# Interleaving the attention of one batch with the feed-forward chunks of the batch before it, and making the v transposes one chunk ahead

## The chip, the cores and the metric

One core of a Trainium2 chip runs the whole program. The metric is the device time in microseconds (us) of one execution, as the median of several. All the executions compared here of one kernel lie within about 0.3% of each other, so differences of a microsecond or two mean something. The profile is one further look at an execution, taken by the hardware profiler; its span (954.9 us for the kernel before) is about 1.5 us shorter than the device time, because it runs from the first to the last instruction.

The engines are PE (matmul), DVE (vector), ACT (scalar, activation functions), POOL (nearly unused here: a broadcast for each batch) and SP, which issues the loads and stores. PSUM is the memory that PE's matmuls write into; copying a result out of it is called evacuation. A *border* is the stretch in which PE finishes one batch's feed-forward and starts the next one's.

## The reference

Cross-covariance attention over channels, then a SwiGLU feed-forward block:

```python
# q, k, v: (4, 6016, 256) float32; tau = 1
qn = q / (norm(q, axis=1) + 1e-6)
kn = k / (norm(k, axis=1) + 1e-6)
s  = kn.transpose(0, 2, 1) @ qn / tau          # 256 x 256 for each of 4 batches
a  = softmax(s, axis=-1)
x  = (v @ a).reshape(24064, 256)
g  = x @ w_gate                                # 256 -> 1536
out = (silu(g) * (x @ w_val)) @ w_out          # 1536 -> 256
```

Two stages follow from it for each batch. *Attention* reads all of q and k (12.3 MB a batch) to form a 256 x 256 matrix of sums (the prediction calls them Gram sums); it moves many bytes and needs few matmuls. *Feed-forward* needs only v, the weights and that matrix; it has many matmuls and moves few bytes. The kernel never forms `v @ a`: it multiplies the softmax into the gate and value weights once per batch ("folding": `awg`, `awv`), so that feed-forward multiplies v by the folded weights.

## The kernel before

Attention for all four batches comes first, in a scope of its own; feed-forward for all four follows. The parts that matter:

```python
# --- stage 1: attention, all batches (weights loaded first, cast to bf16 on DVE) ---
nc.sync.dma_start(wg_f, ...); nc.sync.dma_start(wv_f, ...); nc.sync.dma_start(wo_f, ...)
for b in range(B):
    ktq_ps = attn_psum.tile([P, CB, C], FP32, tag="ktq")      # 2 KB per partition
    diag_ps = attn_psum.tile([P, 4, P], FP32, tag="diag")     # 2 KB per partition
    for ch in range(12):                                       # 512 rows of q and k
        # load qf, kf; cast qt on ACT (L102) and kt on DVE (L103)
        for t in range(nb):                                    # 128 rows: six matmuls
            # 2 x ktq += kt^T qt (256 columns), 4 x diag += qt^T qt, kt^T kt (128 columns)
            ...
    # the chain: diagonal -> sqrt -> 1/norm -> scale -> max -> exp -> softmax a_sb -> transpose aT
    ...
    for (w_sb, aw) in ((wg_sb, awg_all[b]), (wv_sb, awv_all[b])):    # folding
        for ib in range(CB):
            for fo in range(0, F, 512):
                # 2 matmuls of 512 columns into aw_ps, then:
                nc.scalar.copy(aw[:, ib, fo:fo + 512], aw_ps)

# --- stage 2: feed-forward, all batches, chunks of 512 rows ---
def do_chunk(b, n0, nn):
    # load vf, cast vb on ACT
    # 8 transposes of vb into vT_ps (L46), copied to vT by DVE (L213)
    for fb in range(12):
        # 2 matmuls g_ps (L220), 2 matmuls va_ps (L225), 512 columns each
        nc.scalar.activation(sg[:, :nn], g_ps[:, :nn], AF.Silu)
        nc.vector.tensor_mul(hT[:, fb, :nn], sg[:, :nn], va_ps[:, :nn])
    # 48 matmuls o_ps (L240), 256 columns each, copied by ACT, stored
```

The code carries no order between engines: a scheduler in the language orders each engine's instructions, and the engines then run their own lists in order and wait for each other by semaphores.

Of the kernel before, what the change touches and what calls it, by code (L numbers as in the profile page):

```python
# [9 lines left out]
FP32 = mybir.dt.float32  # L10
# [7 lines left out]
def kernel(  # L18
# [19 lines left out]
    QKCH = 512  # L38
    n_full = N // CHUNK
    rem = N - n_full * CHUNK  # L40
# [8 lines left out]
    const = ctx.enter_context(tc.tile_pool(name="const", bufs=1))  # L49
    ident = const.tile([P, P], BF16)  # L50
# [4 lines left out]
    wo_sb = const.tile([P, FB, D], BF16)  # L55

    aw_pool = ctx.enter_context(tc.tile_pool(name="aw", bufs=1))
# [5 lines left out]
    with tc.tile_pool(name="stg", bufs=1) as stg, \  # L63
         tc.tile_pool(name="qkf", bufs=4) as qkf_pool, \
         tc.tile_pool(name="qkb", bufs=4) as qkb_pool, \
         tc.tile_pool(name="attn_psum", bufs=1, space=bass.MemoryType.PSUM) as attn_psum, \
         tc.tile_pool(name="attn_ps2", bufs=2, space=bass.MemoryType.PSUM) as attn_ps2, \
         tc.tile_pool(name="attn_sb", bufs=2) as attn_sb:

        wg_f = stg.tile([P, CB, F], FP32)  # L70
        wv_f = stg.tile([P, CB, F], FP32)
        wo_f = stg.tile([P, FB, D], FP32)
        nc.sync.dma_start(wg_f, moe_w_gate.rearrange("(cb p) f -> p cb f", p=P))
        nc.sync.dma_start(wv_f, moe_w_val.rearrange("(cb p) f -> p cb f", p=P))
        nc.sync.dma_start(wo_f, moe_w_out.rearrange("(fb p) d -> p fb d", p=P))
        nc.vector.tensor_copy(wg_sb, wg_f)
        nc.vector.tensor_copy(wv_sb, wv_f)
        nc.vector.tensor_copy(wo_sb, wo_f)

        nqk = N // QKCH  # L80
        qk_rem = N - nqk * QKCH

        for b in range(B):
            ktq_ps = attn_psum.tile([P, CB, C], FP32, tag="ktq")
            diag_ps = attn_psum.tile([P, 4, P], FP32, tag="diag")

            ti = 0
            for ch in range(nqk + (1 if qk_rem else 0)):
                n0 = ch * QKCH
                nn = min(QKCH, N - n0)  # L90
                nb = nn // P
                qf = qkf_pool.tile([P, 4, C], FP32, tag="qf")
                kf = qkf_pool.tile([P, 4, C], FP32, tag="kf")
                nc.sync.dma_start(  # L94
                    qf[:, :nb, :],
                    q[b, n0:n0 + nn, :].rearrange("(t p) c -> p t c", p=P))
                nc.sync.dma_start(  # L97
                    kf[:, :nb, :],
                    k[b, n0:n0 + nn, :].rearrange("(t p) c -> p t c", p=P))
                qt = qkb_pool.tile([P, 4, C], BF16, tag="qt")  # L100
                kt = qkb_pool.tile([P, 4, C], BF16, tag="kt")
                nc.scalar.copy(qt[:, :nb, :], qf[:, :nb, :])  # L102
                nc.vector.tensor_copy(kt[:, :nb, :], kf[:, :nb, :])  # L103
                for t in range(nb):
                    st = (ti == 0)
                    sp = (ti == N // P - 1)
                    for ci in range(CB):
                        nc.tensor.matmul(  # L108
                            ktq_ps[:, ci, :],
                            kt[:, t, ci * P:(ci + 1) * P], qt[:, t, :],  # L110
                            start=st, stop=sp, skip_group_check=True)
                    for ci in range(CB):
                        nc.tensor.matmul(  # L113
                            diag_ps[:, ci, :],
                            qt[:, t, ci * P:(ci + 1) * P],
                            qt[:, t, ci * P:(ci + 1) * P],
                            start=st, stop=sp, skip_group_check=True)
                    for ci in range(CB):
                        nc.tensor.matmul(  # L119
                            diag_ps[:, 2 + ci, :],  # L120
                            kt[:, t, ci * P:(ci + 1) * P],
                            kt[:, t, ci * P:(ci + 1) * P],
                            start=st, stop=sp, skip_group_check=True)
                    ti += 1

            diag_vals = attn_sb.tile([P, 4], FP32, tag="diagv")
            scratch = attn_sb.tile([P, P], FP32, tag="scratch")
            for s in range(4):
                nc.vector.tensor_tensor_reduce(  # L129
                    out=scratch, in0=diag_ps[:, s, :], in1=ident,  # L130
                    scale=1.0, scalar=0.0, op0=ALU.mult, op1=ALU.add,
                    accum_out=diag_vals[:, s:s + 1])
            normv = attn_sb.tile([P, 4], FP32, tag="normv")
            nc.scalar.activation(normv, diag_vals, AF.Sqrt)
            rnorm = attn_sb.tile([P, 4], FP32, tag="rnorm")
            nc.vector.reciprocal(rnorm, normv)
            rnorm_b = attn_sb.tile([P, 4], BF16, tag="rnorm_b")
            nc.vector.tensor_copy(rnorm_b, rnorm)

            qn_ps = attn_ps2.tile([P, 1024], BF16, tag="attn_post")  # L140
            for ci in range(CB):
                transpose(qn_ps[0:1, ci * P:(ci + 1) * P],
                          rnorm_b[:, ci:ci + 1], ident)
            qn_row = attn_sb.tile([1, C], FP32, tag="qn_row")
            nc.scalar.activation(qn_row, qn_ps[0:1, :C], AF.Copy,
                                 bias=0.0, scale=inv_tau)
            qn_bc = attn_sb.tile([P, C], FP32, tag="qn_bc")
            nc.gpsimd.partition_broadcast(qn_bc, qn_row)  # L148

            a_sb = attn_sb.tile([P, CB, C], BF16, tag="a_sb")  # L150
            for ci in range(CB):
                srow = attn_sb.tile([P, C], FP32, tag="srow")
                nc.scalar.activation(srow, ktq_ps[:, ci, :], AF.Copy,  # L153
                                     bias=0.0, scale=rnorm[:, 2 + ci:3 + ci])
                nc.vector.tensor_mul(srow, srow, qn_bc)
                nsmax = attn_sb.tile([P, 1], FP32, tag="nsmax")
                nc.vector.reduce_max(nsmax, srow, axis=AX.X, negate=True)
                ssum = attn_sb.tile([P, 1], FP32, tag="ssum")
                esr = attn_sb.tile([P, C], FP32, tag="esr")
                nc.scalar.activation(esr, srow, AF.Exp, bias=nsmax,  # L160
                                     accum_out=ssum)
                rsum = attn_sb.tile([P, 1], FP32, tag="rsum")
                nc.vector.reciprocal(rsum, ssum)
                nc.vector.tensor_scalar(a_sb[:, ci, :], esr, rsum,
                                        None, op0=ALU.mult)

            aT_sb = attn_sb.tile([P, CB, C], BF16, tag="aT_sb")
            for cj in range(CB):
                aT_ps = attn_ps2.tile([P, 1024], BF16, tag="attn_post")
                for ci in range(CB):  # L170
                    transpose(aT_ps[:, ci * P:(ci + 1) * P],
                              a_sb[:, ci, cj * P:(cj + 1) * P], ident)
                nc.scalar.copy(aT_sb[:, cj, :], aT_ps[:, :C])

            for (w_sb, aw) in ((wg_sb, awg_all[b]), (wv_sb, awv_all[b])):
                for ib in range(CB):
                    for fo in range(0, F, 512):
                        aw_ps = attn_ps2.tile([P, 512], FP32, tag="attn_post")
                        for jb in range(CB):
                            nc.tensor.matmul(  # L180
                                aw_ps,
                                aT_sb[:, jb, ib * P:(ib + 1) * P],
                                w_sb[:, jb, fo:fo + 512],
                                start=(jb == 0), stop=(jb == CB - 1))
                        nc.scalar.copy(aw[:, ib, fo:fo + 512], aw_ps)  # L185

    with tc.tile_pool(name="v_pool", bufs=3) as v_pool, \
         tc.tile_pool(name="vb_pool", bufs=3) as vb_pool, \
         tc.tile_pool(name="vt_pool", bufs=2) as vt_pool, \
         tc.tile_pool(name="h_pool", bufs=2) as h_pool, \  # L190
# [6 lines left out]
        def do_chunk(b, n0, nn):  # L197
# [11 lines left out]
            for cb in range(CB):  # L209
                for t in range(nb):  # L210
                    transpose(vT_ps[:, cb, t * P:(t + 1) * P],
                              vb[:, t, cb * P:(cb + 1) * P], ident)
# [78 lines left out]
```

## Time and profile before

| | kernel before |
|---|---|
| device time, median | 956.4 us (13 runs, 955.88 to 956.76) |
| span of the profile | 954.9 us |
| first feed-forward matmul | 181.3 us |
| busy: PE, ACT, DVE | 93%, 55%, 49% |
| DMA, 22 to 165 us | full, 349 GB/s to 54 us, then 340 |
| DMA, from 181 us | 58 GB/s |

How to read it: a busy share over the whole span hides that two stages with different limits follow each other. The prediction below shows the slices and windows from which this is read; columns of a window row are its start and end, its length, then for each engine busy time and (x) number of instructions, the granted PE clock, the DMA share and GB/s.

### The profile page before, as it was taken

What the parts mean: (1) busy time and instruction counts of PE and PEld (TensorE: products, weight loads), DVE (VectorE), ACT (ScalarE), POOL (GpSimd) and SP (SyncE); (2) the same over time, 40 slices, a digit from 0 to 9 for tenths busy, and PEclk for the clock granted to TensorE, in tenths of its full rate; (3) what the DMA queues carried; (4) which work ended last, traced back from release to release, by engine and by line L of the source; (5) the groups of instructions that cost most, each with busy time, mean ns of one, the idle gap of its engine ahead of it and who ended that gap; (6) DMA issues with size and microseconds to landing.
All of it is one profiled execution on the core that took longest, in us unless ns stands there. A gap on an engine that the chain in (4) does not pass through costs nothing.

```text
span 954.9 us, 15732 instructions
## 1 busy us (share of the span) xinstructions
PE 886.3 (93%) x6133; PEld 561.1 (59%) x6184; DVE 471.3 (49%) x747; ACT 529.9 (55%) x866; POOL 4.7 (0%) x10
## 2 busy tenths in 40 slices
PE   1777986899999999999999999999999999999998
PEld 1556755465656566656565566556565656565655
DVE  2233232346454555455555645554646454646463
ACT  1375775845564656465555555555556555655454
POOL 0000000000000000000000000000000000000000
PEclk9999998899999999999999999999999999999999
DMA  9999999401220222021202220211122202210011
GB/s 330 349 349 349 347 347 303 117 23 45 62 89 23 89 67 84 23 89 61 85 28 89 67 83 23 90 61 59 52 83 72 76 31 89 62 43 25 23 45 39
DMA packets 101498, 104.30 MB, mean 109 GB/s; under 512 B 3120, under 2 KB 100912, under 8 KB 101424
## 3 DMA queue, kind: packets, MB, share of 16 engines
q1 hardware_dynamic: 101424, 103.30, 34.0%
q8 instruction: 48, 0.79, 0.3%
q14 instruction: 26, 0.21, 0.1%
HBM read 78.64 MB, written 24.64 MB: 108 GB/s over the span
## 4 chain that ended last, share of the span: by engine, by line
PE 79%; issue 12%; DMA 4%; DVE 2%; SPq 2%; ACT 2%; POOL 0%; POOLq 0%; ACTq 0%; DVEq 0%
PE va_ps L225 26%; PE o_ps L240 26%; PE g_ps L220 25%; DMA qf<-in_q_dram 3%; DVE vT L213 2%; SPq L94 1%; PE vT_ps L46 1%; DMA kf<-in_k_dram 1%; SPq L97 0%; ACT vb L205 0%; ACT awg L185 0%; ACT qt L102 0%; ACT awv L185 0%; POOL qn_bc L148 0%; PE aw_ps L180 0%
## 5 line engine op out<-in xcount | busy, mean ns | idle before, releaser
L231 DVE TENSOR_TENSOR hT<-sg,va_ps 128x512 bf16<-128x512 bf16 (+1 forms) x576 | 387.6, 677 | 258.2 <-ACT sg L230 246.9
L230 ACT ACTIVATE sg<-g_ps 128x512 bf16<-128x512 f32 (+1 forms) x576 | 336.8, 589 | 131.4 <-PE g_ps L220 129.4
L225 PE MATMUL va_ps<-vT,awv 128*128 128x512 bf16 (+1 forms) x1152 | 337.4, 374 | 2.4
L220 PE MATMUL g_ps<-vT,awg 128*128 128x512 bf16 (+1 forms) x1108 | 329.2, 374 | 9.3 <-DVE vT L213 7.9
L240 PE MATMUL o_ps<-wo_sb,hT 128*128 128x256 bf16 x2256 | 254.4, 273 | 0.0
L240 PEld LDWEIGHTS <-hT 128*128 128x128 bf16 x2256 | 219.2, 98 | 37.2 <-DVE hT L231 0.5
L225 PEld LDWEIGHTS <-awv 128*128 128x128 bf16 x1152 | 112.5, 98 | 133.6 <-issue 4.3
L220 PEld LDWEIGHTS <-awg 128*128 128x128 bf16 x1152 | 110.7, 98 | 135.7 <-DVE vT L213 11.7
L246 ACT COPY o_sb<-o_ps 128x512 f32<-128x512 f32 x96 | 55.4, 577 | 210.6 <-PE o_ps L240 210.6
L108 PE MATMUL ktq_ps<-qt,kt 128*128 128x256 bf16 x376 | 74.5, 288 | 37.5 <-DVE kt L103 35.8
L102 ACT CAST qt<-qf 128x1024 bf16<-128x1024 f32 (+1 forms) x48 | 49.3, 1028 | 68.3 <-DMA qf<-in_q_dram 68.1
L213 DVE COPY vT<-vT_ps 128x1024 bf16<-128x1024 bf16 (+1 forms) x48 | 30.6, 675 | 102.2 <-PE vT_ps L46 102.2
L103 DVE CAST kt<-kf 128x1024 bf16<-128x1024 f32 (+1 forms) x48 | 33.1, 690 | 88.5 <-DMA kf<-in_k_dram 79.3
L113 PE MATMUL diag_ps<-qt 128*128 128x128 bf16 x376 | 52.6, 226 | 5.6 <-DVE diag_vals L129 4.3
L108 PEld LDWEIGHTS <-kt 128*128 128x128 bf16 x376 | 30.7, 102 | 43.8 <-DVE kt L103 39.3
L119 PE MATMUL diag_ps<-kt 128*128 128x128 bf16 x376 | 54.2, 226 | 1.1 <-DVE kt L103 1.0
L205 ACT CAST vb<-vf 128x1024 bf16<-128x1024 f32 (+1 forms) x48 | 47.4, 1030 | 2.2 <-DMA vf<-in_v_dram 2.0
L113 PEld LDWEIGHTS <-qt 128*128 128x128 bf16 x376 | 35.6, 101 | 14.1 <-ACT qt L102 5.4
L119 PEld LDWEIGHTS <-kt 128*128 128x128 bf16 x376 | 31.8, 102 | 4.6 <-DVE kt L103 1.5
L46 PE MATMUL vT_ps<-ident,vb 128*128 128x128 bf16 x376 | 26.7, 226 | 1.3 <-ACT srow L153 1.2
L46 PEld LDWEIGHTS <-vb 128*128 128x128 bf16 x376 | 24.4, 101 | 2.4 <-issue 1.7
L180 PEld LDWEIGHTS <-aT_sb 128*128 128x128 bf16 x96 | 9.0, 97 | 12.6 <-issue 6.3
(36 smaller groups left out, 110.8 us busy)
## 6 DMA issues: line engine op xcount, KB each, us to landing
qf<-in_q_dram SPq DMA_DIRECT2D x44, 512.0 KB, 8.8
kf<-in_k_dram SPq DMA_DIRECT2D x44, 512.0 KB, 8.8
vf<-in_v_dram SPq DMA_DIRECT2D x44, 512.0 KB, 4.8
out_dram<-o_sb SPq DMA_DIRECT2D x44, 512.0 KB, 3.0
wg_f<-in_moe_w_gate_dram SPq DMA_DIRECT2D x1, 1536.0 KB, 6.9
wv_f<-in_moe_w_val_dram SPq DMA_DIRECT2D x1, 1536.0 KB, 10.7
wo_f<-in_moe_w_out_dram SPq DMA_DIRECT2D x1, 1536.0 KB, 14.7
qf<-in_q_dram SPq DMA_DIRECT2D x4, 384.0 KB, 8.6
```

What stands on the lines that cost most here:

```text
L46: nc.tensor.matmul(out_ap, in_ap, ident_ap, is_transpose=True, start=True, stop=True, skip_group_check=True)
L102: nc.scalar.copy(qt[:, :nb, :], qf[:, :nb, :])
L108: nc.tensor.matmul(ktq_ps[:, ci, :], kt[:, t, ci * P:(ci + 1) * P], qt[:, t, :], start=st, stop=sp, skip_group_check=True)
L113: nc.tensor.matmul(diag_ps[:, ci, :], qt[:, t, ci * P:(ci + 1) * P], qt[:, t, ci * P:(ci + 1) * P], start=st, stop=sp, skip_group_check=True)
L119: nc.tensor.matmul(diag_ps[:, 2 + ci, :], kt[:, t, ci * P:(ci + 1) * P], kt[:, t, ci * P:(ci + 1) * P], start=st, stop=sp, skip_group_chec ...
L213: nc.vector.tensor_copy(vT[:, :, :nn], vT_ps[:, :, :nn])
L220: nc.tensor.matmul(g_ps[:, :nn], awg[:, cb, fb * P:(fb + 1) * P], vT[:, cb, :nn], start=(cb == 0), stop=(cb == CB - 1))
L225: nc.tensor.matmul(va_ps[:, :nn], awv[:, cb, fb * P:(fb + 1) * P], vT[:, cb, :nn], start=(cb == 0), stop=(cb == CB - 1))
L230: nc.scalar.activation(sg[:, :nn], g_ps[:, :nn], AF.Silu)
L231: nc.vector.tensor_mul(hT[:, fb, :nn], sg[:, :nn], va_ps[:, :nn])
L240: nc.tensor.matmul(o_ps[:, t - t0, :], hT[:, fb, t * P:(t + 1) * P], wo_sb[:, fb, :], start=(fb == 0), stop=(fb == FB - 1), skip_group_che ...
L246: nc.scalar.copy(o_sb[:, t0:t1, :], o_ps[:, :t1 - t0, :])
```

## The change

Its intent is to let PE do feed-forward of batch b while the q and k of batch b+1 are loaded, and to take the copy of the transposed v out of PE's path. Its core, cut:

```diff
-        for b in range(B):                      # all of attention first
-            ...                                  # loads, sums, chain, folding
-        for b in range(B):                      # then all of feed-forward
-            for ci in range(n_full):
-                do_chunk(b, ci * CHUNK, CHUNK)
+    for (dst, src, shp) in ((wg_sb, ...), (wv_sb, ...)):   # gate and value weights first
+        ...
+    alloc_attn_state(0)
+    for ch in range(n_ch):
+        attn_qk_chunk(0, ch)
+    ...                                          # output weights loaded here
+    attn_post(0)                                 # chain and folding
+    for b in range(B):
+        nb = b + 1
+        for ch in range(n_ch):
+            mid = nb == B - 1 and ch == n_ch - 2
+            if nb < B - 1:
+                attn_qk_chunk(nb, ch)
+                if ch == n_ch - 1:
+                    attn_post(nb)
+            elif nb == B - 1:                    # last attention: a little faster, so that
+                ...                              # its chain falls before the last chunk
+            ffn_chunk(b, ch, last_qk if mid else None)
```

```diff
 def ffn_chunk(b, ch, between=None):
     ...                                          # 48 gate and value matmuls
+    nxt = (b, ch + 1) if ch + 1 < n_ch else (b + 1, 0)
+    if nxt[0] < B:
+        ffn_vt(*nxt)                             # load, cast, transpose v of the next chunk
+    if between:
+        between()
     ...                                          # 48 output matmuls
```

The kernel's PSUM pools hold eight buffers of 2 KB per partition. Sums keep two, gate and value four, and the remaining two are now shared by the v transposes, output, chain and folding (`ps_misc`); before, each stage had its own.

## The prediction

> **What bounds the kernel now.** I read the page's slices first, to see whether the kernel has one limit or several, then the windows (busy time in chosen stretches) at the borders that the slices show, then the timeline and the waits inside one repeat of each stage. The slices (each 23.9 us):
>
> ```profile
> PE   1777986899999999999999999999999999999998
> PEclk9999998899999999999999999999999999999999
> DMA  9999999401220222021202220211122202210011
> GB/s 330 349 349 349 347 347 303 117 23 45 62 89 23 89 67 84 23 89 61 85 28 89 67 83 23 90 61 59 52 83 72 76 31 89 62 43 25 23 45 39
> ```
>
> There are two regimes. For about seven slices the DMA engines are full at 349 GB/s and PE has holes; for the other 33 PE is full and DMA nearly idle. The windows give the borders (batch 0's Gram sums end near 54, all of attention at 165, the first feed-forward matmul is at 181):
>
> ```profile
> core 0: us, PE busy (x) PEld busy (x) DVE busy (x) ACT busy (x) POOL busy (x), PEclk, DMA share, GB/s
> 22.00:54.00 32.00, 24.02 (x267) 19.67 (x266) 7.50 (x11) 10.30 (x12) 0.00 (x0) 1.00 1.10 349
> 54.00:165.00 111.00, 90.92 (x937) 70.53 (x940) 37.32 (x98) 74.09 (x113) 2.01 (x3) 0.95 1.08 340
> 165.00:181.00 16.00, 11.15 (x61) 6.08 (x63) 3.89 (x12) 14.79 (x28) 0.55 (x1) 0.79 0.72 210
> 181.00:955.00 774.00, 758.46 (x4860) 463.33 (x4903) 416.64 (x622) 427.35 (x715) 0.00 (x0) 1.00 0.18 58
> ```
>
> Attention is bound by loads, feed-forward by PE. Busy PE in the attention stage overstates PE's need, because the ends of its pipelined matmuls are modelled; the pace of work that waits for nothing tells the need. PE's timeline, first in attention, then over two feed-forward chunks:
>
> ```profile
> 151.12 0.38 PE L108 MATMUL ktq_ps<-qt,kt 128*128 128x256 bf16 x2
> 151.56 0.38 PE L108 MATMUL ktq_ps<-qt,kt 128*128 128x256 bf16 x2
> ...
> 305.35 5.40 PE L240 MATMUL o_ps<-wo_sb,hT 128*128 128x256 bf16 x48
> 310.59 1.06 PE L46 MATMUL vT_ps<-ident,vb 128*128 128x128 bf16 x16
> 311.99 0.39 PE L220 MATMUL g_ps<-vT,awg 128*128 128x512 bf16 x1 [0.34 <-DVE vT L213]
> ...
> 322.36 5.40 PE L240 MATMUL o_ps<-wo_sb,hT 128*128 128x256 bf16 x48
> ```
>
> Start to start, one 128-row tile of q and k (six matmuls) takes 151.56 - 151.12 = 0.44 us. The 48 gate and value matmuls of a chunk take 322.36 - 311.99 = 10.37 (0.216 each), the 48 output matmuls 310.59 - 305.35 = 5.24 (0.109 each). The 16 transposes of v, made for two chunks at once, take 1.40 with a wait for DVE's copy that recurs every second chunk:
>
> ```profile
> PE g_ps L220 <- DVE vT L213: 7.9, 22, 0.5
> ```
>
> **What the Trainium skill says.** "Perfetto Trace Analysis", section "Optimization Strategy", says that a kernel whose most-contended engine changes over time may gain from interleaving its regimes: that is this change, and the slices above show the two regimes. "DMA: Bandwidth & Descriptors", section "Where 436 GB/s comes from", gives about 358 GB/s as what HBM allows one core; the trace holds 349, so the loads that come first cannot go faster, only be fewer. "TensorE: Matmul & The Clock Gate", section "Wait — 56ns, not 53.3ns?", gives warm spacings of 55.6 ns at 128 columns and 215.7 ns at 512; the trace has 216 at 512, so feed-forward matmuls have no slack and only waits and order can be gained. "ScalarE: Activation LUTs", section "What ACT_TABLE_LOAD costs", gives 1283 ns for a change of function table and another 1380 of drain; the trace agrees on the first and shows no drain of that size (a load began 0.03 us after the cast ahead of it):
>
> ```profile
> L134 ACT ACT_TABLE_LOAD x4 | 5.1, 1283 | 0.1
> L160 ACT ACT_TABLE_LOAD x4 | 5.1, 1283 | 0.1
> L185 ACT CAST awg<-aw_ps 128x512 bf16<-128x512 f32 x24 | 13.1, 601 | 2.2 <-PE diag_ps L119 1.0 <-PE aw_ps L180 0.7 <-PE aT_ps L46 0.5
> ```
>
> **The change, part by part.** I read where instructions land from the built order of each engine, before and after.
>
> *Start.* Only batch 0's attention now precedes feed-forward, and the output weights are loaded after it. That takes 1.57 MB / 349 GB/s = 4.5 us from in front: batch 0's sums end at 54.6 - 4.5 = 50.1. Then come its softmax chain and folding. In the last batch before, these show as
>
> ```profile
> 161.86 0.29 DVE L129 CUSTOM_DVE_ANT_0 scratch<-diag_ps,ident 128x128 f32<-128x128 f32 x1 [1.48 <-PE diag_ps L119]
> 171.48 1.23 PE L180 MATMUL aw_ps<-wg_sb,aT_sb 128*128 128x512 bf16 x3
> 181.31 0.61 PE g_ps L220 x2
> ```
>
> (the last line is from the chain in order of time): 19.5 us from sums to first gate matmul. In the new order ACT casts the fourth q chunk of batch 1 before the first Silu, so the loads set this point: after batch 0's last k (about 47.9) come 1.57 MB of weights, 3.67 of q and k and 2.10 of v, 7.34 MB / 349 = 21.0 us, giving 68.9; plus a cast (1.04) and a table load (1.28), 71.3. The first matmul comes just before, so I put feed-forward's start at 71 for 181.3: **-110.3**.
>
> *Moved on to PE's path.* Three batches of 47 tiles are 141 x 0.44 = 62.0 us; 74 matmuls (12.3 tiles, 5.4 us) stand in or before the first feed-forward chunk, where PE waits for loads or ACT anyway, leaving 56.6. Folding is 3 x 24 matmuls x 0.216 = 15.6, small transposes 1.0. Together **+73.2**. The loads behind them are hidden: a chunk of 17.8 us (10.37 + 5.24 + 0.44 + 1.76) moves 2.1 MB, 6 us at 349.
>
> *The transposes of v* now stand between a chunk's gate and output matmuls, so DVE's copy runs beside the output matmuls. A pair took 1.40 and needs 16 x 0.055 = 0.88: 0.52 x 23 pairs, **-12**.
>
> *Batch borders.* For batches 1 and 2 the chain runs while PE does the old batch's last chunk (384 columns) and about four chunks of q and k of the batch after next. PE's work there is 112 x 0.073 + 48 x 0.162 + 24 x 0.216 + 36 x 0.109 + transposes = about 26 us. ACT's is 12 folding evacuations (7.2), 12 Silus (5.9), four table loads (5.1), four q casts (4.2), scaling and Exp (2.7) and small copies (3), 28 us, in strict order with PE and DVE through two shared PSUM buffers. Walking through the built order with the durations above, the last output matmul ends 31 us after the start, so 5.5 us lost at each. The last border hides its chain under output matmuls and I put it at 4. Together with 1 in the first chunk, **+16**.
>
> Sum: 956.4 - 110.3 + 73.2 - 12 + 16 = 923.3, say 924 us, 3.4% less.
>
> **The rivals.** *The borders are much dearer.* For it: ACT has two q casts, four evacuations and a Silu between steps that PE waits on, PE runs in order, and transposes, folding and output now share two buffers. If nothing overlapped, a border would cost the 19.5 us above instead of the roughly 5.5 of PE work plus 5 lost that I count: about 27 us more, 951. Against it: the built order does put feed-forward and q/k matmuls into those waits. A middle outcome is 935 to 940.
>
> *A wait for loads takes the place of the old one.* The one DMA queue is in order, and a store waiting for its output tile stands before later loads. A stall of 1 us in each of about 30 chunks would give 954. Against it: the order issues q, k and v several chunks ahead, four load buffers stand behind three cast buffers, and DMA has two thirds of each chunk free.
>
> *ACT or DVE becomes the bound of a mixed chunk.* ACT has 12 x 0.60 + 2 x 1.05 + 2 x 0.59 = 10.5, DVE 12 x 0.69 + 0.69 + 0.70 = 9.7 of 17.8 us: I give it little.
>
> *Better than I count:* borders fully hidden give 908.
>
> **Range and chances.** The start (4 us either way) and the borders (10 less to 15 more) carry the error, the borders lopsidedly upward: 912 to 941. The 2% line is 937.3; below it would take border losses of twice my figure plus a late start, or a systematic load wait, to miss: faster 0.82, within 2% 0.16, slower 0.02.
>
> **What would show each step.** Feed-forward's first Silu near 71 us and DMA full only until about 80. Mixed chunks of 17.8 us and unmixed ones of 16.05, PE's wait for the vT copy gone, granted clock 1.0 from 80 on. Around the two first borders (near 265 and 480) a dip in PE over about 31 us, with ACT close to full, and a smaller dip near 690. I am wrong if mixed chunks exceed 18.3, if PE's q/k matmuls wait on casts or loads after 90 us, if a border loses over 10 us, or if feed-forward begins after 76.

## The result, and the profile after

The changed kernel takes 914.7 us (median of 8 runs, 914.07 to 915.08), the kernel before 956.41 on the same chip. The ratio is 0.9564, with a 95% interval of 0.9554 to 0.9573: 4.4% faster. Such a ratio is taken from the means of the runs, so it is not quite the ratio of the quoted medians.

The slices of the changed kernel (each 22.8 us), then its windows:

```profile
PE   3669999999999999999999999999999999999998
PEclk9989999999999999999999999999999999999999
DMA  9998433423346123334334522221121122120111
GB/s 328 349 340 287 136 96 117 140 93 116 125 130 202 47 73 125 93 111 134 121 100 156 156 93 81 70 65 47 47 72 68 42 70 70 52 83 24 36 35 41
```

```profile
core 0: us, PE busy (x) PEld busy (x) DVE busy (x) ACT busy (x) POOL busy (x), PEclk, DMA share, GB/s
22.00:50.00 28.00, 19.70 (x228) 15.75 (x226) 6.20 (x10) 10.48 (x10) 0.00 (x0) 1.00 1.10 349
50.00:72.00 22.00, 14.29 (x103) 8.96 (x106) 8.35 (x24) 17.02 (x30) 1.37 (x1) 0.84 1.06 340
72.00:85.00 13.00, 12.79 (x75) 6.53 (x74) 9.35 (x15) 11.66 (x18) 0.00 (x0) 1.00 1.05 336
85.00:913.00 828.00, 819.02 (x5680) 521.91 (x5725) 438.56 (x696) 492.49 (x810) 1.65 (x3) 1.00 0.28 91
```

The stretch before the first feed-forward matmul shrank from 181 us to 72 (loads run at full rate until about 85); the rest is PE's at full granted clock, and the loads of the next batches are spread under it (91 GB/s in place of 58). One mixed chunk, in PE's timeline (start, length, engine, line, operation):

```profile
140.84 0.38 PE L233 MATMUL g_ps<-vT,awg 128*128 128x512 bf16 x1
151.23 0.61 PE L44 MATMUL vT_ps<-ident,vb 128*128 128x128 bf16 x8
151.68 5.40 PE L258 MATMUL o_ps<-wo_sb,hT 128*128 128x256 bf16 x48
156.92 0.38 PE L114 MATMUL ktq<-qt,kt 128*128 128x256 bf16 x2
158.68 0.38 PE L233 MATMUL g_ps<-vT,awg 128*128 128x512 bf16 x1
```

Gate and value take 151.23 - 140.84 = 10.39 us, the transposes 0.45, output 5.24 and the sums of q and k 158.68 - 156.92 = 1.76, without a gap between them: 17.84 us. No wait of PE for the copy of vT is left; that line, 7.9 us before, is absent among PE's waits.

### The profile page after: what moved, and what is told of

The parts are those of the page before. It is cut to its first block, busy times and chain, and to the rows that moved or that the text cites. A ratio compares the mean times of both kernels' runs of the same rounds, so it can differ in the third digit from the quotient of the medians.

```text
span 913.0 us, 15682 instructions
## 1 busy us (share of the span) xinstructions
PE 871.9 (95%) x6133; PEld 558.4 (61%) x6184; DVE 468.1 (51%) x747; ACT 536.1 (59%) x871; POOL 4.9 (1%) x10
## 4 chain that ended last, share of the span: by engine, by line
issue 71%; PE 23%; DMA 4%; SPq 1%; ACT 1%; DVE 0%; POOL 0%; POOLq 0%; DVEq 0%; ACTq 0%
PE va_ps L238 7%; PE o_ps L258 7%; PE g_ps L233 7%; DMA qf<-in_q_dram 2%; DMA kf<-in_k_dram 2%; SPq L100 1%; PE aw_ps L191 1%; PE vT_ps L44 1%; POOL qn_bc L160 0%; SPq L102 0%; ACT L243 0%; ACT qt L106 0%; DVE scratch L134 0%; ACT esr L172 0%; SPq L78 0%
## 5 line engine op out<-in xcount | busy, mean ns | idle before, releaser
L114 PE MATMUL ktq<-qt,kt 128*128 128x256 bf16 x376 | 73.0, 279 | 24.4 <-DVE kt L107 24.3
L208 ACT CAST vb<-vf 128x1024 bf16<-128x1024 f32 (+1 forms) x48 | 49.6, 1034 | 11.1 <-PE vT_ps L44 11.0
L118 PE MATMUL diag<-qt 128*128 128x128 bf16 x376 | 52.4, 223 | 3.8 <-ACT qt L106 3.7
L123 PE MATMUL diag<-kt 128*128 128x128 bf16 x376 | 53.0, 223 | 0.1
L44 PE MATMUL vT_ps<-ident,vb 128*128 128x128 bf16 x376 | 28.8, 219 | 0.0
```

The source lines that it names most:

```text
L44: nc.tensor.matmul(out_ap, in_ap, ident_ap, is_transpose=True, start=True, stop=True, skip_group_check=True)
L114: nc.tensor.matmul(st_.ktq_ps[:, ci, :], kt[:, t, ci * P:(ci + 1) * P], qt[:, t, :], start=s0, stop=s1, skip_group_check=True)
L118: nc.tensor.matmul(st_.diag_ps[:, ci, :], qt[:, t, ci * P:(ci + 1) * P], qt[:, t, ci * P:(ci + 1) * P], start=s0, stop=s1, skip_group_chec ...
L123: nc.tensor.matmul(st_.diag_ps[:, 2 + ci, :], kt[:, t, ci * P:(ci + 1) * P], kt[:, t, ci * P:(ci + 1) * P], start=s0, stop=s1, skip_group_ ...
L208: nc.scalar.copy(vb[:, :nb, :], vf[:, :nb, :])
```

## The experiments

Every run below gave a correct result. The kernel before ran beside them at 956.36 to 956.40 us, so medians can be compared directly. "After" is the changed kernel, 914.7 us.

### 1. All of attention first again

The changed kernel with its order of stages undone and all else kept.

```diff
-    for b in range(B):
-        nb = b + 1
-        ...                                      # interleaved
+    for b in range(1, B):
+        alloc_attn_state(b)
+        for ch in range(n_ch):
+            attn_qk_chunk(b, ch)
+        attn_post(b)
+    for b in range(B):
+        for ch in range(n_ch):
+            ffn_chunk(b, ch)
```

> The changed kernel with all of attention first again, as before, but with its other parts kept (pools, transposes of v one chunk ahead). It splits the gain of 41.7 us. Theory A (regimes overlapped, with the sizes of the prediction): what is left here is the 12 us of the transposes plus about 12 us of the last batch's chain and folding, which the built order now lays beside the first feed-forward chunk; so about 932 us, and interleaving proper is worth about 17. Rival B (the transposes and the shared scope alone make the gain): about 915 us. Rival C (only interleaving counts): about 954 us. Unmixed chunks should take 16.05 us.

Measured: 934.6 us (ratio 0.9772). Theory A's 932 is close; both rivals fall. Of the gain of 41.7 us, interleaving proper is 934.6 - 914.7 = 19.9, and 21.8 come without it. The next experiment splits these.

### 2. The kernel before with only the transposes ahead

```diff
-        def do_chunk(b, n0, nn):                 # load, cast, transpose v; then the rest
+        def make_vt(b, n0, nn):                  # load, cast, transpose v
+            ...
+        def do_chunk(b, n0, nn, nxt):
             ...                                  # gate and value matmuls
+            if nxt:
+                make_vt(*nxt)
             ...                                  # output matmuls
```

> The kernel before with one edit: each chunk's transposes of v made between the previous chunk's gate and output matmuls; nothing is interleaved, pools as before. The prediction gave this part 12 us, the traces of before and after suggest 13 to 14 (chunks of 16.05 us in place of pairs of 32.6). Theory A: the part stands on its own, 942 to 944 us. Rival B: it is worth this only in the changed kernel's shared pools and order, and here the end is the same or only 5 us earlier, 951 to 956.

Measured: 942.1 us (ratio 0.9852), 14.2 us faster than before. Theory A holds: this part stands on its own, and is worth a little more than the 12 us of the prediction. PE's wait for the vT copy is gone here too. Together with experiment 1, the gain of 41.7 us can be laid out as 14.2 (transposes) + 7.6 (what is left of 21.8) + 19.9 (interleaving). The 7.6 are a remainder and were not tested alone. They fit what the trace of experiment 1 shows: the last batch's chain and folding run beside the first chunk, as all stages now share one scope, and that chunk is complete at 189.9 us, where before it was at 198.1. The split also depends on the order in which the parts are added, as the next experiment shows.

### 3. The changed kernel without transposes ahead

```diff
-        nxt = (b, ch + 1) if ch + 1 < n_ch else (b + 1, 0)
-        if nxt[0] < B:
-            ffn_vt(*nxt)
```

> The changed kernel with the transposes of v made at the head of their own chunk. Theory A (they save a wait of about 0.5 us per pair of chunks everywhere): 12 to 14 us slower than the changed kernel, 927 to 929. Rival B (in mixed chunks the built order puts q/k matmuls between the transposes and the gate matmuls, which hides the copy, so only the last batch's 12 chunks pay 0.5 us each): 6 us slower, about 921, as long as the borders stay as they are. The built order here puts no gate matmuls into the borders' chain; if that exposes it, each of two borders loses 5 us more, 931.

Measured: 940.9 us (ratio 0.9837), 26.2 us slower than after: more than any branch gave. PE's timeline in the last batch, where nothing is mixed in:

```profile
752.04 0.61 PE L44 MATMUL vT_ps<-ident,vb 128*128 128x128 bf16 x8
753.43 0.38 PE L233 MATMUL g_ps<-vT,awg 128*128 128x512 bf16 x1 [0.78 <-DVE vT L216]
```

From transposes to gate matmul 1.39 us pass, for every chunk. The kernel before paid 1.40 for *two* chunks, because it transposed two at once; here a chunk takes 17.0 us in place of 16.05. That is 11.5 us over the last batch (the delay against after grows from 14.7 to 26.2 us there), twice what rival B counted. In mixed chunks q/k matmuls do stand between the two, as B said. The other 14.7 us arise up to the end of batch 2; I did not split them further. This run also differs in more than the copy's wait, because the scheduler laid q/k matmuls differently (126 of them start between 260 and 280 us, against 80 in the changed kernel). What follows: the two parts of the change help each other. The transposes alone give 14.2 us (experiment 2), the rest alone 956.4 - 940.9 = 15.5, both together 41.7, so 12.0 come only with both. A likely reason, not tested by itself, is that without transposes ahead no gate matmuls of the next chunk can fill the borders: PE's waits after 84 us add up to 17.9 us here, 10.1 of them for the copy of vT, against 1.7 in the changed kernel.

### 4. Output weights loaded first

```diff
+    wtmp = stg.tile([P, 3072], FP32, tag="wtmp")      # moved up, unchanged
+    nc.sync.dma_start(..., moe_w_out...); nc.vector.tensor_copy(wo_sb, ...)
     alloc_attn_state(0)
     for ch in range(n_ch):
         attn_qk_chunk(0, ch)
-    wtmp = stg.tile(...)
-    nc.sync.dma_start(..., moe_w_out...); nc.vector.tensor_copy(wo_sb, ...)
     attn_post(0)
```

> The changed kernel with the output weights loaded at the very start again. Theory A (by the time of the first Silu the same bytes must have landed in either order, because q casts of batch 1 stand before it on ACT): 0 to 1 us slower, 915. Rival B (the 4.5 us by which batch 0's sums end earlier go through to the end): 4.5 us slower, 919. Rival C (the weights stand before batch 1's first q and k, which the built order puts before the transposed softmax on PE, so the late load costs as much as it saves): 0 to 2 us faster.

Measured: 918.9 us (ratio 0.9609), 4.2 slower than after. Rival B holds and theory A, which was a step of my prediction, falls. The first Silu, in ACT's timeline of the changed kernel and then of this one:

```profile
74.56 1.09 ACT L243 ACTIVATE sg<-g_ps 128x512 bf16<-128x512 f32 x2
```

```profile
79.48 1.08 ACT L243 ACTIVATE sg<-g_ps 128x512 bf16<-128x512 f32 x2
```

A delay of 4.5 us in front goes through: 4.9 us at the first Silu, 4.2 at the end. The bytes that must land before the first Silu are nearly the same in both orders, so it is not the loads of batch 1 that set the start, but batch 0's sums and what follows from them.

### 5. The last border made like the others

```diff
-            mid = nb == B - 1 and ch == n_ch - 2
-            if nb < B - 1:
+            mid = False
+            if nb < B:
                 attn_qk_chunk(nb, ch)
                 if ch == n_ch - 1:
                     attn_post(nb)
-            elif nb == B - 1:
+            elif False:
-        own = b == B - 1
+        own = False
```

> The changed kernel with the last border made like the first two (one q/k chunk per chunk, chain before the last chunk of batch 2, the shared buffers), so without its special place under the output matmuls. No q/k matmuls of a further batch are left to fill that chain. Theory A (the chain takes about 10 us from sums to folding and only 5.5 us of gate and value matmuls stand beside it): 4 to 5 us slower, 919. Rival B (borders cost little whatever their form, as the first two lost only 2.4 us each): within 1 us, 915.

Measured: 919.4 us (ratio 0.9617), 4.7 slower than after. Theory A holds. PE's waits in this border add up to 4.8 us, against 1.4 in the changed kernel. The first two borders have 112 matmuls of q and k to fill such waits; the last has none beyond its own, and gains from its place under the output matmuls. (The edit changes the place, the spread of q and k and the PSUM buffers together; which of them counts most was not separated.)

### 6. Half of folding's evacuations on DVE

```diff
-                    nc.scalar.copy(aw[:, ib, fo:fo + 512], aw_ps)
+                    if (fo // 512 + ib) % 2:
+                        nc.vector.tensor_copy(aw[:, ib, fo:fo + 512], aw_ps)
+                    else:
+                        nc.scalar.copy(aw[:, ib, fo:fo + 512], aw_ps)
```

> The changed kernel with half of the 12 evacuations of each folding moved from ACT to DVE. Theory A (ACT's strict order is what the borders and batch 0's folding wait for): ACT sheds 6 evacuations, about 3 us, at each of four foldings; the 2.4 to 2.6 us lost at each of three borders shrink to about 1, and feed-forward starts about 2 us earlier: 4 to 6 us faster than the changed kernel, 909 to 911. Rival B (what is lost is the latency of the chain, in which PE runs in order, and ACT has room): within 1 us of it, 914 to 916.

Measured: 913.4 us (ratio 0.9552), 1.3 us faster than after; the intervals of the two ratios overlap, though the runs themselves (913.27 to 913.89, against 914.07 to 915.08) do not. A's 4 to 6 us are refuted. By PE's timeline the first border takes 27.17 us here, with 14 q/k matmuls fewer in it (1.0 us): 2.3 us lost in place of 2.6; the last takes 26.73 in place of 26.83. What is lost at the borders is not ACT's throughput. Most of the small gain lies at the start, where the first gate matmul comes at 70.58 us in place of 71.96.

### 7. All weights after batch 0's q and k

Since experiment 4 had shown that a load before batch 0's sums is paid almost in full (4.2 of 4.5 us), the gate and value weights should go behind them too; they are needed only at folding.

```diff
-    for (dst, src, shp) in ((wg_sb, ...), (wv_sb, ...)):     # load and cast
-        ...
     alloc_attn_state(0)
     for ch in range(n_ch):
         attn_qk_chunk(0, ch)
+    for (dst, src, shp) in ((wg_sb, ...), (wv_sb, ...)):
+        ...
+    attn_post(0)
     ...                                          # output weights, as before
-    attn_post(0)
```

> The changed kernel with gate and value weights too loaded after batch 0's q and k (then the output weights). Theory A (the run of loads 41.0 had refuted that loads set feed-forward's start: it is batch 0's sums plus its chain): 3.15 MB / 349 GB/s = 9 us come out from in front, the weights land while the chain runs, and the first Silu comes at 64 to 66 in place of 74.6; but only 33 q/k matmuls of batch 1 then stand before the end of the first chunk in place of 74, and 41 x 0.073 = 3 us come back on PE: 907 to 909. Rival B (the weights are needed at folding, so the bytes before folding are the same in both orders): within 2 us of the changed kernel, 913 to 916.

("The run of loads 41.0" in this text is a slip of mine for experiment 4.)

Measured: 908.7 us (ratio 0.9503), 6.0 faster than after, within A's 907 to 909. The first gate matmul comes at 64.3 us in place of 72.0, and some of that is paid back, because fewer sums of batch 1 are done by then: 33 q/k matmuls stand before the end of the first chunk in place of 74.

### 8. Late weights and split evacuations together

This is experiment 6 with a variant of 7: the output weights are loaded after batch 1's first q and k.

```diff
+    attn_post(0, cast_gate_val)                  # weights loaded just before, cast before folding
...
+                if b == 0 and ch == 0:
+                    load_wo()
```

> Both together (weights after batch 0's q and k, the output weights after batch 1's first q and k; half of folding's evacuations on DVE). If both theories A hold the gains add, apart from the folding of batch 0: 903 to 906. If only the late weights count: 907 to 909. If neither: 914.

Measured: 908.2 us (ratio 0.9497), 0.5 below experiment 7, with overlapping intervals. The late weights make the gain; what the other two edits add is too small to tell apart here. PE's timeline shows the next limit, a wait for the softmax (`a_sb`) at the start:

```profile
49.90 0.86 PE L44 MATMUL aT_ps<-ident,a_sb 128*128 128x128 bf16 x4 [5.68 <-DVE a_sb L166]
```

### 9. Two weight casts on POOL

```diff
-            nc.vector.tensor_copy(
+            (nc.vector if dst is wg_sb else nc.gpsimd).tensor_copy(
                 dst, wtmp.rearrange("p (a b) -> p a b", a=CB))
...
-        nc.vector.tensor_copy(wo_sb, ...)
+        nc.gpsimd.tensor_copy(wo_sb, ...)
```

> The last kernel (weights late, evacuations split) with the casts of the value and output weights moved from DVE to the idle POOL. In its trace the cast of the value weights (1.74 us) stood on DVE between the Exp and the scaled softmax, and PE waited 5.7 us there for the softmax. Theory A (batch 0's chain sets the start): the chain is 1.7 us shorter and another 1.75 us of DVE go from the folding: 1.5 to 3 us faster, 905 to 907. Rival B (POOL is slower at the cast, or the evacuations then wait for loads of batch 1): no change or slower, 908 to 910. Borders as before.

Measured: 908.2 us (ratio 0.9497), no change; A falls. POOL's cast takes 2.74 us, where DVE's took 1.74. The timelines of POOL and DVE show where the 1.7 us that DVE was spared went:

```profile
47.63 2.74 POOL L282 CAST wv_sb<-wtmp 128x3072 bf16<-128x3072 f32 x1 [1.33 <-DMA wtmp<-in_moe_w_val_dram]
```

```profile
48.30 2.23 DVE L166 TENSOR_SCALAR a_sb<-esr,rsum 128x256 bf16<-128x256 f32 x1
```

The scaling of the softmax takes 0.34 us in experiment 8, where POOL is idle, and 2.23 here. It starts while POOL casts and ends at 50.53, just after POOL's cast (47.63 + 2.74 = 50.37). The Trainium skill, "SBUF — State Buffer", section "Who interferes with whom", says that POOL and some forms of DVE's copy, cast and tensor_scalar hold a shared pair of memory ports exclusively, so that the later one waits for the whole instruction. This trace agrees with that: the long DVE instruction ends with POOL's cast, and the next scaling, at 50.63, takes 0.35 us again.

### 10. Keeping PE busy while it waits for batch 0's chain

```diff
+        if b == 0:
+            warm_ps = ps_gv.tile([P, CHUNK], FP32, tag="g_ps", name="warm_ps")
+            for _ in range(90):
+                nc.tensor.matmul(warm_ps[0:4, :P], rnorm_b, ident,
+                                 start=True, stop=True, skip_group_check=True)
```

> The late-weights kernel (x8) with 90 small matmuls on PE after batch 0's norms, whose result nobody reads. In x8 PE idles 5.7 us there, and the granted clock is 0.50 from 48 to 54 us, so that the first folding matmuls take twice as long. Theory A (the half clock costs 2 us at the start): granted clock near 1 there, 1 to 2.5 us faster than 908.2. Rival B (the evacuations and loads set the pace of folding anyway): within 0.7 us.

Measured: 906.1 us (ratio 0.9475), 2.1 us faster than experiment 8, as A said. (The 95% intervals of the two ratios just touch, 0.9484 to 0.9510 and 0.9462 to 0.9488; the runs, 908.12 to 908.71 and 906.08 to 906.30, do not overlap.) One window row of experiment 8, then the same of this one (the third number from the end is the granted clock):

```profile
48.00:54.00 6.00, 3.89 (x14) 1.70 (x15) 3.64 (x6) 2.60 (x7) 0.00 (x0) 0.50 1.10 348
```

```profile
48.00:54.00 6.00, 4.83 (x48) 2.93 (x45) 3.94 (x8) 3.37 (x8) 0.00 (x0) 1.00 1.10 350
```

With the idle time filled, PE keeps its full clock. Of the 48 matmuls in the second row, 28 are the filler itself, so the counts do not show what was gained. The folding matmuls do: first those of experiment 8, then the filler and the folding of this one, in PE's timelines:

```profile
51.12 2.74 PE L184 MATMUL aw_ps<-wg_sb,aT_sb 128*128 128x512 bf16 x6
```

```profile
44.34 5.19 PE L150 MATMUL warm_ps<-ident,rnorm_b 128*4 128x128 bf16 x90
51.34 1.09 PE L189 MATMUL aw_ps<-wg_sb,aT_sb 128*128 128x512 bf16 x4 [0.30 <-ACT aT_sb L180]
```

Six take 2.74 us at the half clock, four take 1.09 at the full one, and the first gate matmul comes at 61.23 us in place of 62.79. This is the best version found: 5.3% below the kernel before, 0.9% below the change.

## Why the prediction was right, and where it was off

The time, 914.7 us, lies in the range (912 to 941), and "faster by over 2%" was right; the central figure of 924 was 9.3 us too high. Step by step, with the terms as measured:

| term | predicted, us | measured, us | from |
|---|---|---|---|
| start of feed-forward | -110.3 | -109.3 | first gate matmul 181.31 to 71.96 |
| first chunk | +1 | +0.7 | 84.56 - 71.96 = 12.60 less four output matmuls (0.44), 11.43 before |
| PE work moved in | +73.2 | +73.2 | same counts (772 q/k matmuls after 84.56); a mixed chunk adds 1.79 |
| transposes of v | -12 | -14.2 | experiment 2 |
| borders | +15 | +7.8 | three times 2.6 |
| sum from 956.4 | 923.3 | 914.6 | measured 914.7 |

**Two regimes, one hidden under the other: right.** Experiment 1 shows it. Mixed chunks take 17.84 us and unmixed ones 16.05, as predicted, with the granted clock at 1.00 from 72 us on. No load wait took the old one's place: PE's waits for q and k casts lie before 85 us. That rival falls, and so does the one of a saturated ACT or DVE: between 103 and 172 us, in mixed chunks, they are busy for 39.9 and 37.3 of 69 us.

**Start of feed-forward: right in size, wrong in reason; that the size agrees within 1 us is luck.** I let the loads of batch 1 set it (71 us; the first gate matmul came at 71.96). Experiments 4 and 7 refute that reason: 4.5 us more in front cost 4.2 at the end, and weights moved behind the sums gained 6.0. What sets it is batch 0's sums and then the chain and folding. That ACT's list, in which q and v casts stand between folding's evacuations, has a part in it is only suggested: taking half the evacuations off ACT brought the first gate matmul 1.4 us forward (experiment 6). The first Silu, which I had put at 71.3, came at 74.56. PE runs the matmuls just before folding at half clock: the granted clock was 0.50 from 54 to 60 us, and 1.00 from 60 us, where folding begins.

**Borders: a loss, as predicted, but wrong in size and in part in reason.** This is the term that made the error, 7 of 9 us. I took ACT's work there as 28 us, adding up durations, and walked through the order with them, arriving at 31 us and 5.5 lost. (31 less my 26 is 5, not 5.5; and the terms given for the first Silu add up to 71.2, not 71.3. Neither slip matters.) PE's timeline at the first border, first and last row of it and the next chunk:

```profile
263.96 0.38 PE L114 MATMUL ktq<-qt,kt 128*128 128x256 bf16 x2
...
288.30 4.09 PE L258 MATMUL o_ps<-wo_sb,hT 128*128 128x256 bf16 x36
292.44 0.38 PE L233 MATMUL g_ps<-vT,awg 128*128 128x512 bf16 x1
```

It lasts 292.44 - 263.96 = 28.48 us against 25.9 us of PE work: 2.6 lost. The second border, from 481.43 to 509.91, lasts as long. ACT's timeline in the first, and the group row of the same evacuation (busy time, mean ns of one):

```profile
283.25 1.17 ACT L196 CAST awv<-aw_ps 128x512 bf16<-128x512 f32 x2
284.22 1.14 ACT L106 CAST qt<-qf 128x1024 bf16<-128x1024 f32 x1
285.17 1.17 ACT L196 CAST awv<-aw_ps 128x512 bf16<-128x512 f32 x2
```

```profile
L196 ACT CAST awv<-aw_ps 128x512 bf16<-128x512 f32 x24 | 13.9, 657 | 0.3 <-PE aw_ps L191 0.2
```

Two evacuations start to start take 284.22 - 283.25 = 0.97 us, 0.49 each, though one is recorded with 0.657; a q cast is followed after 0.95, though recorded with 1.14. Instructions in a row overlap by 0.1 us and more, which over some 40 of them is, by estimate, 4 us or more that I had counted twice. ACT's busy time in this border, with overlaps counted once, is 25.63 of the 28.48 us. The Trainium skill, "ScalarE: Activation LUTs", section "What ACT_TABLE_LOAD costs", gives an overlap of about 93 ns for ACTIVATEs in a row; the casts above show 0.17 and 0.19 us. I had read the section and not used it. So ACT was close to full, as I said, but it did not set the pace: with six evacuations taken off it, the border lost only 0.3 us less (experiment 6). What the remaining 2.6 us are made of (many waits of 0.1 to 0.3 us through two shared PSUM buffers and the chain) was seen but not tested.

**The last border** has its special form for a reason, and I gave it 4 us: it lost 2.6 (26.83 us for 24.2 of PE work), and its plain form would have lost 4.7 more (experiment 5).

**Transposes: right, a little small.** 14.2 in place of 12. I had counted the wait and the difference in transposes of 23 pairs; the rest was not followed up. That the measured terms add up to within 0.1 us should not be read as proof of each: the 14.2 come from the kernel before, and experiment 3 shows that the same part is worth 26.2 in the changed kernel.

## What to carry to other kernels

Where a load-bound stage precedes a PE-bound one, interleave them batch by batch, and compute the gain as the time until the second stage may start, less PE work moved into it; then look at what stays bare in front: loads that needn't be there cost 4.2 of their 4.5 us in experiment 4, and moving 9 us of loads away gave back 6.0 in experiment 7. Size a busy stretch by the spacing from start to start, not by adding recorded durations. Give each serial chain other independent work in the in-order list of the engine that waits for it, and check that an idle start hasn't halved the clock of what follows.

## What the Trainium skill lacked or had wrong

- "ScalarE: Activation LUTs", section "What ACT_TABLE_LOAD costs": it adds about 1380 ns of drain to a change of table. Here a load begins 0.03 us after the cast ahead of it, and the next function follows 0.01 us after the load's 1.283 us; no such drain is seen.
- "TensorE: Matmul & The Clock Gate", section "Back-to-back issue gap": it gives, for streams of weight loads and matmuls, about 131 ns at 512 columns and 81 ns at 128. Here such streams run at 216 ns and 55 ns, the figures which the page calls isolated.
- No page says whether matmuls that use only a few columns of the array are enough to keep the clock ("TensorE: Matmul & The Clock Gate" would be the place): in experiment 10, 90 matmuls with a stationary operand of 4 columns, 5.19 us in all, held it at 1.00, where an idle stretch of 5.7 us had left 0.50 for the next matmuls.
